# Float phases and mirrored-token sums on GpSimd, constants in parts: one change to a fused S4 convolution and GEGLU kernel

## The chip, the cores and the metric

The kernel runs on one core of a Trainium2 chip. The metric is the device time of one execution in microseconds, as a median of several runs. Engines are called by their names in the profile: PE is TensorE, DVE is VectorE, ACT is ScalarE, POOL is GpSimd, SP is SyncE, whose queue issues nearly all DMAs.

## What is computed

Two branches read the same tokens u (2048 tokens, 640 channels, bf16) and are mixed by a gate.

```python
def _A_ref(u, A_re, A_im, B_re, B_im, C_re, C_im, log_dt, Dskip):
    dt = jnp.exp(log_dt)[:, None]
    A, Bc, Cc = A_re + 1j * A_im, B_re + 1j * B_im, C_re + 1j * C_im
    P = jnp.exp((dt * A)[:, :, None] * l[None, None, :])
    K = jnp.einsum("dn,dnl,dn->dl", Cc, P, dt * Bc).real
    ...
    return y + u * Dskip[None, None, :]

def _B_ref(x, w_gate, w_up, w_down):
    return (_gelu(x @ w_gate) * (x @ w_up)) @ w_down

g = _sigmoid((x * gate_w).sum(-1, keepdims=True))
return g * a + (1 - g) * b
```

The part left out is the causal convolution y of u with K over 2048 lags, by Fourier transforms; l is 0 to 2047, rounded to bf16. A_re and the other parameters are 640 x 128; the feed-forward width is 1728.

## The kernel before, in words

The channels are worked in two halves of 320, the tokens of the feed-forward branch in two halves of 1024.

**Tables of K.** K at lag l is a sum over 128 states of a complex exponential. Each lag is written as a lag from a list of 21 ("a", `PQ`) plus a multiple of 8 up to 8 x 31 ("b", `B2`), and K comes from a product of the two tables on PE (`contract`, L515 and L516, jobs `ct`). An entry needs a magnitude (an exponential on ACT, steps `xa`, `xb`) and a cosine and a sine. The angle is built in chunks of three multiples: `phase_b` (L475) writes `th * 8m` as a 32-bit integer, of which 65536 is a full turn (step `fb`); `ph_q` (L462) reads its low 16 bits, adds a quarter turn, and writes a second integer; ACT's sine (L485 in `sin_b`, step `sb`) reads both; DVE multiplies sine and cosine by the magnitude (L503 in `prod_b`, steps `pb`, `pc`). The "a" table has the same steps: L467, L462, L479 and L494 (`fa`, `sa`, `pa`). Six b chunks (five of three multiples, one of a single one) and seven a chunks make one half of the channels. The integers live in a buffer `ph` of two slots, so a chunk's phase waits until the sine of the chunk two before has read its slot.

**Mirrored tokens.** The convolution is done in four blocks of 512 tokens by matmuls with cosine and sine matrices. For each block the tokens 256 to 511 are loaded as they are (`uf`, L354, on SP) and the tokens 255 to 0 in reverse by two indirect DMAs on POOL (`ur`, L358). The sum and the difference (L365, steps `uf0.0`, `uf0.1` and so on, bf16, 128 x 1280) go to `pm0`, which SP stores to DRAM (L366, step `us`); halves of it are loaded later (`lu`, L716). There is one `uf`, one `ur` and one `pm0`, so each block waits for the one before.

**Constants.** The matrices FM (for u, 512 KB), KMa and KMb (for K, 1 MB and 512 KB) and IM (inverse, 512 KB) are loaded by one DMA each on SP: `lfm`, `lkm`, `lkm2`, `lim`. PE uses them in L691 (jobs `U`), L704 (jobs `K`) and L764 (jobs `I`), a column block m of 128 at a time.

**Feed-forward.** PE multiplies weights with transposed tokens (L374, ten matmuls a job, jobs `g`, `u`), into one of four PSUM tiles; ACT or DVE evicts (L379, L381). Up values are spilled to DRAM through a ring of three slots (L401) and come back later (L679). Weights come through two slots of `Wr` (L270, L271 on SP). GELU, products and the down projection (L779) follow in the second part.

**What orders the work.** A string `ORDER`, written out, lists all steps; each engine and queue carries out its own instructions in that order, one after the other, and a wait holds up everything behind it. The program's names: `work`, `early` and `tail` are large SBUF buffers in which the small ones are laid out (`early` holds `uf`, `ur`, `pm0`, later FM and KMa; `work` holds `ph`).

Of the kernel before, what the change touches and what calls it, by code (L numbers as in the profile page):

```python
# [31 lines left out]
LATE = (8, 9, 10, 11)  # L32
UF = (("Uf0", "Uf1", "Uf2", "Uf3"), ("Ub0", "Uf0", "Uf1", "Uf2"))
# [6 lines left out]
al2 xb19.0 lp3 fb0.0 xb3.0 x3.0 xb11.0 xb15.0 fb1.0 xb14.0 x0.0 xb10.0 xb29.0 x1.0 xb23.0 xb21.0 xb7.0 xb9.0 lw1 t3/0  # L40
xb31.0 ur0 c3 t5/1 leu0 t4/2 x3.1 v3 xb2.0 xb12.0 v2 xa3.0 ul0 v1 xb17.0 x1.1 xa4.0 v0 xb5.0 g1.0/3 xa15.0 v5 xb13.0
leu1 x0.1 v4 xa14.0 xa8.0 u1.0/0 v6 eg1.0/D x2.1 v7 xa19.0 v8 lgw xa10.0 leu3 xa1.0 u0.0/1 eu1.0/D lsk xa9.0 v9 v11
uf0.1 xa17.0 g0.0/2 xb25.0 eu0.0/D xa5.0 v10 xb1.0 uf0.0 su1.0 xa7.0 xb4.0 v12 g2.0/3 us0 xa11.0 ur1 xb8.0 eg0.0/D
xa16.0 lw2 v13 g3.0/0 eg2.0/A x4.1 fil.0 mag v14 ma5.0 ul1 v15 ma2.0 su0.0 u3.0/1 eg3.0/A leu2 ma3.0 lu00 ma1.0 v16
ma0.0 tabT ma4.0 u2.0/2 ma6.0 v17 sb0.0 v18 u4.0/3 lw3 eu2.0/A pb0.0 sb1.0 su2.0 pc0.0 g4.0/0 uf1.0 eu3.0/A pc1.0
eu4.0/A g5.0/2 su3.0 uf1.1 at su4.0 pb1.0 us1 ur2 eg4.0/A ul2 fb2.0 gl/1 eg5.0/A fb3.0 sb2.0 u5.0/3 ph45 gl1 sb3.0
pc2.0 g6.0/0 pb2.0 lw4 eu5.0/A pb3.0 su5.0 g7.0/2 fb4.0 eg6.0/A pc3.0 sb4.0 u6.0/1 uf2.1 uf2.0 eg7.0/A fb5.0 us2 ur3
fa0.0 g8.0/3 ul3 sb5.0 eu6.0/A pb4.0 su6.0 u7.0/0 eg8.0/A pc4.0 fa1.0 sa0.0 u8.0/2 lw5 pb5.0 eu7.0/A pa0.0 u9.0/1
# [47 lines left out]
def constants():  # L96
# [37 lines left out]
    return b(fm), b(im), b(km), b(picks)  # L134


@with_exitstack
def kernel(
# [322 lines left out]
    def ph_q(t, n):  # L461
        ts(out=t[:, 1, 0:n], in0=low16(t[:, 0, 0:n])[:, :, ::2], scalar1=TURN / 4, scalar2=None, op0=ALU.add)  # L462
# [400 lines left out]
```

## Time and profile before

| | |
|---|---|
| Median of 3 runs | 295.86 us (294.83 to 297.05) |
| Profiled execution, its own time | 296.23 us |
| Its span in the profile | 294.4 us, so 1.8 us lie around it |
| Mean granted TensorE clock | 0.965 |
| POOL | 15.2 us busy in 23 instructions |

A busy row of a view gives start, duration, engine, line, operation, output <- input, shapes and count; the bracket at its end is the idle time of that engine just before, with what ended it. A row of a group gives total and mean of one. The line numbers L are those of the kernel before. A window row gives length, then for PE, PEld (weight loads), DVE, ACT and POOL the busy time and the number of instructions, then the granted clock, the share of DMA and GB/s. A label SPq is the issuing of a DMA on SP's queue.

### The profile page before, as it was taken

The numbers are of one execution on the slowest core, as the hardware profiler recorded it, in microseconds if no ns is written. First come the engines' busy times: TensorE is split into PE (matmuls) and PEld (weight loads), VectorE is DVE, ScalarE is ACT, GpSimd is POOL, SyncE is SP. The second block draws the span as 40 slices with busy tenths as digits, with TensorE's granted clock in tenths as the row PEclk, the third lists the DMA queues.
The fourth block names the chain that finished last, engine by engine and source line by source line (L and its number), as shares of the span: only waits on it lengthen the run. The fifth ranks groups of instructions, "written<-read, shape, count | busy, mean of one in ns | idle before, by whom it ended". The sixth has DMA issues, their size and how long they took to land.

```text
span 294.4 us, 4960 instructions
## 1 busy us (share of the span) xinstructions
PE 265.4 (90%) x1883; PEld 161.0 (55%) x1883; DVE 268.4 (91%) x352; ACT 215.8 (73%) x308; POOL 15.2 (5%) x23
## 2 busy tenths in 40 slices
PE   6399799999999799997098999999999999999994
PEld 4344354444584344443076446677767677677762
DVE  1599999999979879999997999999999999999993
ACT  3999978799989969999989998963764554304301
POOL 4103030200100000000001000000000000000000
PEclk9779999999999979999579999999999999999999
DMA  7996997754787893285769777844401200011001
GB/s 202 230 217 152 266 362 233 250 162 117 234 231 185 230 295 113 92 267 173 231 143 296 247 224 205 286 143 131 116 24 28 63 22 22 13 34 47 22 22 45
DMA packets 63149, 46.94 MB, mean 159 GB/s; under 512 B 23276, under 2 KB 53527, under 8 KB 62999
## 3 DMA queue, kind: packets, MB, share of 16 engines
q1 hardware_dynamic: 62166, 44.90, 54.3%
q0 software_dynamic: 384, 1.31, 1.3%
q10 hardware_dynamic: 576, 0.43, 0.5%
q8 instruction: 14, 0.23, 0.3%
q14 instruction: 9, 0.07, 0.1%
HBM read 29.39 MB, written 14.62 MB: 149 GB/s over the span
## 4 chain that ended last, share of the span: by engine, by line
DVE 63%; PE 17%; DMA 8%; ACT 4%; issue 4%; SPq 2%; ACTq 0%; DVEq 0%
DVE work L750 11%; PE ps L374 11%; DVE work L749 11%; DVE work L746 7%; DVE work L381 4%; DVE work L494 4%; DVE work L503 4%; DVE work L467 4%; DMA Wr<-in_B_w_up_dram 3%; DVE work L462 3%; DVE H L680 2%; DVE work L680 2%; DVE work L752 2%; PE ps L515 2%; PE ps L516 2%
## 5 line engine op out<-in xcount | busy, mean ns | idle before, releaser
L374 PE MATMUL ps<-xT,Wr 128*128 128x512 bf16 x540 | 121.9, 386 | 4.8 <-DMA Wr<-in_B_w_up_dram 1.9
L374 PEld LDWEIGHTS <-Wr 128*128 128x128 bf16 x540 | 53.1, 99 | 69.3 <-issue 7.4
L379 ACT CAST work<-ps 128x640 bf16<-128x640 f32 (+2 forms) x54 | 44.4, 838 | 36.3 <-PE ps L764 22.2
L750 DVE TENSOR_TENSOR work<-work 128x2560 bf16<-128x2560 bf16 x24 | 35.7, 1487 | 0.4
L779 PE MATMUL ps<-xT,work 128*128 128x320 bf16 x224 | 31.6, 299 | 0.1
L779 PE MATMUL ps<-xT,H 128*128 128x320 bf16 x224 | 31.2, 299 | 0.0
L479 ACT ACTIVATE tail<-work 128x1920 bf16<-128x1920 int16 x14 | 25.3, 1807 | 2.5 <-DVE work L503 1.7
L779 PEld LDWEIGHTS <-work 128*128 128x128 bf16 x224 | 21.9, 98 | 8.9 <-issue 0.3
L779 PEld LDWEIGHTS <-H 128*128 128x128 bf16 x224 | 21.8, 98 | 8.5
L503 DVE TENSOR_TENSOR work<-tail,work 128x1920 bf16<-128x1920 bf16 (+1 forms) x22 | 23.2, 1092 | 0.6 <-ACT tail L485 0.6
L515 PE MATMUL ps<-work 128*128 128x84 bf16 x160 | 14.1, 210 | 9.9 <-DVE work L494 9.9
L385 ACT ACTIVATE Wr<-ps,gs 128x320 bf16<-128x320 f32 x29 | 13.6, 535 | 12.4 <-PE ps L787 7.5
L485 ACT ACTIVATE tail<-work 128x960 bf16<-128x960 int16 (+1 forms) x24 | 20.7, 915 | 0.5 <-DVE work L475 0.4
L381 DVE CAST work<-ps 128x1024 bf16<-128x1024 f32 (+2 forms) x16 | 17.1, 1070 | 3.9 <-PE ps L374 2.7
L764 PE MATMUL ps<-work,tail 128*128 128x320 bf16 x128 | 19.5, 300 | 1.2 <-DVE work L431 0.6
L516 PEld LDWEIGHTS <-work 128*128 128x128 bf16 x160 | 13.6, 103 | 10.6 <-issue 10.4
L467 DVE SCALAR_TENSOR_TENSOR work<-tail 128x320 int32<-128x320 f32 x42 | 18.0, 484 | 0.0
L462 DVE TENSOR_SCALAR work<-work 128x960 int32<-128x960 int16 (+1 forms) x26 | 16.5, 636 | 1.1
L764 PEld LDWEIGHTS <-tail 128*128 128x128 bf16 x128 | 12.2, 98 | 7.2 <-issue 1.8
L691 PEld LDWEIGHTS <-early 128*128 128x128 bf16 x128 | 12.4, 98 | 6.8 <-issue 1.4
L494 DVE TENSOR_TENSOR work<-tail,work 128x1920 bf16<-128x1920 bf16 x14 | 16.0, 1152 | 0.0
L691 PE MATMUL ps<-work,early 128*128 128x320 bf16 x80 | 13.6, 299 | 1.2 <-DVE work L381 1.2
(121 smaller groups left out, 411.9 us busy)
## 6 DMA issues: line engine op xcount, KB each, us to landing
Ud<-work SPq DMA_DIRECT2D x22, 256.0 KB, 2.0
work<-Ud SPq DMA_DIRECT2D x22, 256.0 KB, 3.0
Wr<-in_B_w_gate_dram SPq DMA_DIRECT2D x12, 320.0 KB, 7.1
Wr<-in_B_w_up_dram SPq DMA_DIRECT2D x12, 320.0 KB, 4.4
PMd<-early SPq DMA_DIRECT2D x4, 640.0 KB
Gd<-work SPq DMA_DIRECT2D x9, 256.0 KB, 2.0
work<-Gd SPq DMA_DIRECT2D x9, 256.0 KB
out_dram<-Wr SPq DMA_DIRECT2D x14, 160.0 KB, 1.9
```

Of the source, the lines that this page charges most:

```text
L374: P.matmul(t[:, x, :], lhsT=Wr[:, slot, kt, cols:cols + 128], rhs=xT[:, th, kt, 512 * x:512 * x + 512], start=(kt == 0), stop=(kt == 4))
L379: A.copy(out=out, in_=in_)
L381: V.tensor_copy(out=out, in_=in_)
L462: ts(out=t[:, 1, 0:n], in0=low16(t[:, 0, 0:n])[:, :, ::2], scalar1=TURN / 4, scalar2=None, op0=ALU.add)
L467: stt(out=t[:, 0, x], in0=at["th"][:, d], scalar=float(A_OF[3 * c + x] + MID), in1=at["ph45"][:, d], op0=ALU.mult, op1=ALU.add)
L494: tt(out=PQ[:, :, 3 * c:3 * c + 3].rearrange("p r x d -> p x r d"), in0=T.rearrange("p r x d -> p x r d"), in1=e[:, :, None, :].to_broadca ...
L503: tt(out=B2[:, :, :, cols].rearrange("p r g x -> p g r x"), in0=Tv if hf == 0 else Tv[:, :, ::-1], in1=e, op=ALU.mult)
L691: P.matmul(t[:, r, 0:W2], lhsT=FM[:, e, r, 128 * m:128 * m + 128], rhs=pm[:, r, e], start=(e == 0), stop=(e == 1))
L749: step(f"m{h}{c}{i}{part}", lambda ux=ux, kx=kx: tt(out=fl(t), in0=ux, in1=kx, op=ALU.mult))
L750: step(f"s{h}{c}{i}{part}", lambda dst=dst, op=op: tt(out=fl(dst), in0=fl(dst), in1=fl(t), op=op))
L764: P.matmul(t[:, r, 0:W2], lhsT=IM[:, m, r, 128 * e:128 * e + 128], rhs=Y[:, r, m], start=(m == 0), stop=(m == 3))
L779: P.matmul(t[:, x, 0:W2], lhsT=H[c // 2][:, ft, tk:tk + 128], rhs=at[f"Wd{h}"][:, ft], start=(ft == 0), stop=False)
```

## The change

Three things change; every other step keeps its place in the list.

1. `phase_b` is split: its float part runs on POOL (`G.tensor_scalar` in place of DVE's `ts`), 16 instructions of 128 x 320 for each half of the channels. The integer part `ph_q` becomes a step of its own (`qb`, and `qa` for the a chunks, whose float part stays on DVE), directly behind `fb` or `fa`.
2. The sums and differences of mirrored tokens run on POOL (`G.tensor_tensor`), 8 instructions of 128 x 1280.
3. The constants are laid out anew on the host so that a column block is contiguous, and each load becomes several: FM 4, KMa 4, KMb 2, IM 2. These 12 DMAs stand where the 4 stood. The matmuls read the same numbers at new places.

```diff
@@ ORDER
-al2 xb19.0 lp3 fb0.0 xb3.0 x3.0 xb11.0 xb15.0 fb1.0 xb14.0 x0.0 xb10.0 xb29.0 x1.0 xb23.0 xb21.0 xb7.0 xb9.0 lw1 t3/0
+al2 xb19.0 lp3 fb0.0 qb0.0 xb3.0 x3.0 xb11.0 xb15.0 fb1.0 qb1.0 xb14.0 x0.0 xb10.0 xb29.0 x1.0 xb23.0 xb21.0 xb7.0
...
+eu12.1/D xa15.1 xa3.1 xa5.1 su12.1 xa7.1 ma1.1 xa16.1 g0.1/2 lfm0 lfm1 lfm2 lfm3 eg13.1/D kt.0 xb14.1 xa10.1 eu13.1/D
+xa19.1 xb23.1 xb4.1 ma2.1 xb2.1 xb1.1 eg0.1/D su13.1 g1.1/1 xb13.1 xb10.1 ma5.1 sg0.1 xb6.1 ma3.1 lka0 lka1 lka2 lka3
...
@@
         for r, op in ((0, ALU.add), (1, ALU.subtract)):
-            step(f"uf{c}.{r}", lambda c=c, r=r, op=op: tt(out=at["pm0"][:, r], in0=at["uf"], in1=at["ur"], op=op))
+            step(f"uf{c}.{r}", lambda c=c, r=r, op=op: G.tensor_tensor(out=at["pm0"][:, r], in0=at["uf"], in1=at["ur"], op=op))
@@ phase_b
         for x in range(n):
-            ts(out=t[:, 0, x], in0=at["th"][:, d], scalar1=8.0 * (3 * c + 1 + x), scalar2=TURN / 8, op0=ALU.mult, op1=ALU.add)
-        ph_q(t, n)
+            G.tensor_scalar(out=t[:, 0, x], in0=at["th"][:, d], scalar1=8.0 * (3 * c + 1 + x), scalar2=TURN / 8,
+                            op0=ALU.mult, op1=ALU.add)
@@ tables
+                step(f"qa{c}.{h}", lambda t=t: ph_q(t, 3))
...
+                step(f"qb{c}.{h}", lambda t=t, n=n: ph_q(t, n))
@@ loads
-    step("lfm", lambda: S.dma_start(out=at["FM"], in_=FMd))
-    step("lkm", lambda: S.dma_start(out=at["KMa"], in_=KMd[:, 0:4096]))
+    for m in range(4):
+        step(f"lfm{m}", lambda m=m: load_part("FM", FMd, m, 512))
+    for m in range(4):
+        step(f"lka{m}", lambda m=m: load_part("KMa", KAd, m, 1024))
...
+    def load_part(name, src, x, n):
+        S.dma_start(out=at[name][:, n * x:n * x + n], in_=src[:, n * x:n * x + n])
@@ u_mm
-                P.matmul(t[:, r, 0:W2], lhsT=FM[:, e, r, 128 * m:128 * m + 128], rhs=pm[:, r, e], start=(e == 0),
+                P.matmul(t[:, r, 0:W2], lhsT=FM[:, m, e, r], rhs=pm[:, r, e], start=(e == 0),
                          stop=(e == 1))
```

The compiled order shows where the moved instructions stand. In the rows of the change the line numbers are those of the changed file: L480 is `phase_b`, L364 the indirect loads, L371 the sums, L468 `ph_q`, L508 `prod_b`, L564 the step `ph45`, L603 `load_part`.

POOL's queue from its last early memset on, before:

```order
L585 MEMSET skip 32x640
L595 MEMSET H_78 64x1024
L358 DMA early<-in_A_u_dram,back 128x640 x8
L655 MEMSET xT 64x320
L543 MEMSET work 128x320
```

and the same place now:

```order
L606 MEMSET H_78 64x1024
L480 TENSOR_SCALAR work<-tail 128x320 x6
L364 DMA early<-in_A_u_dram,back 128x640 x2
L371 TENSOR_TENSOR early<-early 128x1280 x2
L364 DMA early<-in_A_u_dram,back 128x640 x2
L371 TENSOR_TENSOR early<-early 128x1280 x2
L364 DMA early<-in_A_u_dram,back 128x640 x2
L480 TENSOR_SCALAR work<-tail 128x320 x9
L371 TENSOR_TENSOR early<-early 128x1280 x2
L480 TENSOR_SCALAR work<-tail 128x320
L364 DMA early<-in_A_u_dram,back 128x640 x2
L371 TENSOR_TENSOR early<-early 128x1280 x2
```

The eight indirect loads, alone in the queue before, now alternate with the sums that read them, and the phases of chunks 2 to 5 stand between.

DVE in the first half of the channels, from the first b products to the single phase of chunk 5, before:

```order
L503 TENSOR_TENSOR work<-tail,work 128x80x2x12 x2
L365 TENSOR_TENSOR early<-early 128x1280
L503 TENSOR_TENSOR work<-tail,work 128x80x2x12
L365 TENSOR_TENSOR early<-early 128x1280
L503 TENSOR_TENSOR work<-tail,work 128x80x2x12
L475 TENSOR_SCALAR work<-tail 128x320 x3
L462 TENSOR_SCALAR work<-work 128x960
L475 TENSOR_SCALAR work<-tail 128x320 x3
L462 TENSOR_SCALAR work<-work 128x960
L559 TENSOR_SCALAR tail<-work 128x640
```

and now:

```order
L508 TENSOR_TENSOR work<-tail,work 128x80x2x12 x4
L468 TENSOR_SCALAR work<-work 128x960 x2
L564 TENSOR_SCALAR tail<-work 128x640
L508 TENSOR_TENSOR work<-tail,work 128x80x2x12 x3
L468 TENSOR_SCALAR work<-work 128x960
L508 TENSOR_TENSOR work<-tail,work 128x80x2x12
L468 TENSOR_SCALAR work<-work 128x320
```

The sums and float phases are gone from between the products; the integer phases stay where they were and take their input from POOL.

SP's queue where FM and KMa are loaded, now (before, both rows of constants were one DMA each, of 128 x 2048 and 128 x 4096):

```order
L407 DMA Ud_68<-work 128x1024
L603 DMA early<-fm_c 128x512 x4
L541 DMA KTt<-Kd_70 32x5x320 x4
L543 DMA edge_k<-Kd_70 4x320
L543 DMA edge_k<-Kd_70 6x320
L543 DMA edge_k<-Kd_70 4x320
L407 DMA Ud_68<-work 64x1024
L407 DMA Gd<-work 128x1024
L603 DMA early<-ka_c 128x1024 x4
L407 DMA Gd<-work 64x1024
```

Three issues are added ahead of K's way back from DRAM and the next spills, three more behind them.

More of the change, by code (lines that the diff above doesn't have):

```diff
@@ L44 @@
[L44 to L48, printed above, removed]
@@ L601 @@
     step("hz1", lambda: G.memset(H[1][64:128, 13], 0.0))
[L602 to L603 removed]
+    for m in range(2):
+        step(f"lkb{m}", lambda m=m: load_part("KMb", KBd, m, 1024))
+    for e in range(2):
+        step(f"lim{e}", lambda e=e: load_part("IM", IMd, e, 1024))
     def gate_mm():
```

112 lines of the change are left out of this document (59 added, 53 removed).

## The prediction, made blind

> **What bounds the kernel now.** I read the page first: the engines' busy shares and the split of the chain of waits.
>
> ```profile
> PE 265.4 (90%) x1883; PEld 161.0 (55%) x1883; DVE 268.4 (91%) x352; ACT 215.8 (73%) x308; POOL 15.2 (5%) x23
> DVE 63%; PE 17%; DMA 8%; ACT 4%; issue 4%; SPq 2%; ACTq 0%; DVEq 0%
> ```
>
> By the average, DVE is the bound and POOL is empty, so work moved from DVE to POOL ought to pay. That average hides the stages, so next come busy times by stage, for the two stretches in which the tables of K are made (first half of the channels, second half) and for the end.
>
> ```profile
> 57.30:86.20 28.90, 28.31 (x264) 16.06 (x263) 27.30 (x49) 27.59 (x27) 1.05 (x2) 1.00 0.63 183
> 109.20:147.30 38.10, 28.63 (x138) 13.36 (x137) 37.65 (x62) 36.78 (x38) 0.00 (x0) 0.91 0.57 180
> 250.00:286.00 36.00, 35.51 (x262) 25.35 (x260) 35.42 (x27) 9.18 (x18) 0.00 (x0) 1.00 0.09 28
> ```
>
> The columns after the length are PE, PEld, DVE, ACT and POOL. Where the changed work lies, three engines are full together in the first stretch, and DVE and ACT in the second (ACT idle 38.10 - 36.78 = 1.3 us). At the end PE and DVE are both full, so a lag that arrives there stays. PE's timeline says the same:
>
> ```profile
> 44.30 34.69 PE L374 MATMUL ps<-xT,Wr 128*128 128x512 bf16 x160
> 79.58 0.20 PE L515 MATMUL ps<-work 128*128 128x84 bf16 x1 [0.59 <-DVE work L494]
> 147.65 0.23 PE L515 MATMUL ps<-work 128*128 128x84 bf16 x1 [9.28 <-DVE work L494]
> ```
>
> From 44.30 to 78.99 PE runs 160 matmuls without a gap, 2.17 us for each ten. At both places where the tables end, PE waits for DVE's last product (L494): 0.59 us and 9.28 us. Faster DVE work in the first half can win at most the 0.59; in the second half it must also pass ACT, whose own waits for DVE there are these three, 1.1 us in all:
>
> ```profile
> 127.02 1.80 ACT L479 ACTIVATE tail<-work 128x1920 bf16<-128x1920 int16 x1 [0.57 <-DVE work L503]
> 135.26 1.80 ACT L479 ACTIVATE tail<-work 128x1920 bf16<-128x1920 int16 x1 [0.26 <-DVE work L462]
> 144.16 1.80 ACT L479 ACTIVATE tail<-work 128x1920 bf16<-128x1920 int16 x1 [0.26 <-DVE work L462]
> ```
>
> **The change part by part.** It takes 32 float phases (L475) and 8 sums (L365) off DVE.
>
> ```profile
> L475 DVE TENSOR_SCALAR work<-tail 128x320 int32<-128x320 f32 x32 | 8.5, 320 | 0.0
> L365 DVE TENSOR_TENSOR early<-early 128x1280 bf16<-128x1280 bf16 x8 | 6.5, 820 | 0.4 <-DMA early<-in_A_u_dram 0.3
> ```
>
> DVE is freed of 8.5 + 6.5 = 15.0 us. No row shows POOL doing arithmetic. Its nearest are memsets, one written stream:
>
> ```profile
> 0.94 0.35 POOL L544 MEMSET work<- 128x320 bf16 x1
> 2.48 0.95 POOL L595 MEMSET H<- 64x1024 bf16 x1
> ```
>
> The slope is (0.95 - 0.35)/704 = 0.85 ns an element. A phase on 320 elements costs at least 0.35 us, and at most 0.70 if read and write follow one another; I take 0.5. A sum on 1280 elements costs at least 0.35 + 960 x 0.85 ns = 1.17 us for one stream, at most 3.5 for three streams in turn; I take 2.3, the two inputs in turn, since the rows give a price for a stream and two must be read. POOL so gets 32 x 0.5 + 8 x 2.3 = 34.4 us of work.
>
> [...]
>
> *First sums.* They replace DVE work that begins at 23.08; the store that needs them, at the head of SP's queue, is the second row.
>
> ```profile
> 23.08 0.83 DVE L365 TENSOR_TENSOR early<-early 128x1280 bf16<-128x1280 bf16 x1
> 28.06 0.36 SPq L366 DMA_DIRECT2D PMd<-early  x1
> ```
>
> Starting then, POOL ends at 23.1 + 4.6 = 27.7, ahead of 28.06: nothing. At 3.5 us each it would end at 30.1, and the weight loads behind it in SP's queue would slip 2 us.
>
> *POOL's queue.* The order on POOL is fb0, fb1, load, sums, load, sums, load, then fb2 to fb4. So fb2, needed by the integer phase (L462) early in the table, stands behind the second sums and the third indirect load, and both loads that follow sums also wait for them. These rows give the clock of that queue:
>
> ```profile
> 37.83 0.83 DVE L365 TENSOR_TENSOR early<-early 128x1280 bf16<-128x1280 bf16 x1 [0.29 <-DMA early<-in_A_u_dram]
> 40.73 1.62 POOL L358 DMA_INDIRECT early<-in_A_u_dram,back  x1 [11.54 <-DVE early L365]
> 42.66 1.10 POOL L358 DMA_INDIRECT early<-in_A_u_dram,back  x1 [0.30 <-issue]
> 42.27 0.66 DVE L462 TENSOR_SCALAR work<-work 128x960 int32<-128x960 int16 x1
> 43.41 1.90 ACT L485 ACTIVATE tail<-work 128x960 bf16<-128x960 int16 x2
> 47.05 1.01 ACT L379 CAST work<-ps 128x1024 bf16<-128x1024 f32 x1
> early<-in_A_u_dram,back POOLq DMA_INDIRECT x8, 5.6
> ```
>
> The second sums can't start before their data land at 37.8. Two take until 42.4; the pair of indirect loads follows 0.3 later (POOL's own step in the third row) and takes 3.03: 45.7; fb2 three times 0.5: 47.2; DVE's integer phase 0.66: 47.9, where it ended at 42.93. DVE, relieved of three phases and two sums, reaches this point near 40 (42.27 - 0.8 - 1.6) and stands: behind it are L559 and the products L503. ACT's sine, at 43.41 in the row, starts at 47.95, 4.5 late, and the eviction behind it (47.05 in the row) ends at 52.6. PE has four PSUM tiles and wants this one back for its fifth tile, at 44.30 + 4 x 2.17 = 53.0: just covered, with 0.4 us left, so the stall goes to ACT and DVE and not yet to PE.
>
> The next knot is the single fb5 behind the third sums. fb4 waits for the sine's read (49.85) and ends at 51.35; the third loads, issued by 44.6, have landed (5.6 us) by 50.2; sums to 55.95; fb5 56.45; integer phase 56.8.
>
> ```profile
> 52.84 0.35 DVE L462 TENSOR_SCALAR work<-work 128x320 int32<-128x320 int16 x1
> 57.40 1.80 ACT L479 ACTIVATE tail<-work 128x1920 bf16<-128x1920 int16 x1 [1.10 <-DVE work L503]
> 57.44 0.38 SPq L271 DMA_DIRECT2D Wr<-in_B_w_up_dram  x1
> ```
>
> Before, it ended at 53.19: DVE is 3.6 late although it was freed of six phase groups and six sums. ACT's first joint sine, which waited for DVE in the row, starts 3.6 late. From there ACT can make up about 0.3 us (of the 1.3 idle in its stretch, part is a wait for PE's products), so PE's table products at 79.58 start **3.3 us late**. The store of the third sums slips to 56.0 in SP's queue, but the weight load behind it waits for PE until 57.44 anyway: nothing. The last pair of sums and fb0, fb1 of the second half have POOL to themselves: nothing, as long as they end inside ACT's lag.
>
> With the low prices the same steps end at 52.4, 0.8 early, of which PE can use 0.59: -0.6. With the high ones they end at 63.0: +9.8.
>
> *PE's restart.* The gap before 79.58 grows from 0.59 to about 4 us.
>
> ```profile
> 101.03 0.70 PE L691 MATMUL ps<-work,early 128*128 128x320 bf16 x4 [1.17 <-DVE work L381]
> 102.74 4.00 PE L374 MATMUL ps<-xT,Wr 128*128 128x512 bf16 x10 [1.01 <-DVE work L381]
> 109.03 2.32 PE L374 MATMUL ps<-xT,Wr 128*128 128x512 bf16 x10
> ```
>
> After gaps of 1.17 and 1.01 us, ten matmuls took 4.00 us instead of 2.32. So such a gap can cost 0 to 1.7 us: +0.8.
>
> *Second half.* Ten phases inside the stretch from 109.20 leave DVE (10 x 0.27 = 2.7 us). POOL has an empty queue, so they are ready. ACT's waits of 1.1 us are all that can be won: 0 to -1.1, I take -0.6.
>
> *Constants in parts.* Eight more issues on SP.
>
> ```profile
> 93.46 0.32 SPq L597 DMA_DIRECT2D early<-fm_c  x1
> 93.83 1.86 SPq L536 DMA_DIRECT2D KTt<-Kd  x4
> 95.74 1.00 SPq L538 DMA_DIRECT2D edge_k<-Kd  x3
> 97.21 0.49 SPq L401 DMA_DIRECT2D Ud<-work  x1
> 99.75 1.22 DVE L381 CAST work<-ps 128x1024 bf16<-128x1024 f32 x1 [0.18 <-DMA Ud<-work]
> 98.61 1.25 PE L691 MATMUL ps<-work,early 128*128 128x320 bf16 x8
> 158.39 0.91 SPq L666 DMA_DIRECT2D work<-Gd  x2
> 160.23 0.32 SPq L679 DMA_DIRECT2D work<-Ud  x1
> ```
>
> ```profile
> 173.46 0.43 SPq L603
> 173.98 0.58 SPq L716
> ```
>
> Three more issues of about 0.4 at 93.46 use up the 0.47 free before 97.21 and push that spill by 0.7; the cast at 99.75 waits for it, and PE for the next cast. +0.7 (0 to 1.7, if the three of KMa add to it). No wait gets shorter: U000 (98.61) waits for no load, and the first K product is K003, which needs the last part of KMa. The last fence is from the chain of waits, which at 173.46 runs through SP's queue; there is one issue more: +0.4 (0 to 0.45). The part of KMb goes in just before 158.39, and the gap of 0.9 before 160.23 takes it up: nothing.
>
> Sum: 3.3 + 0.8 - 0.6 + 0.7 + 0.4 = **+4.6 us** on the profiled execution's 296.23 (0.4 above the median of 295.86): **300.8 us**.
>
> **The rivals.** *Low prices, no change:* -0.6 + 0 - 0.6 + 0.7 + 0.4 = -0.1, 296.1. For it: only POOL's memsets are shown, and they are quick. Against: two operands.
>
> *Faster:* DVE alone is the bound. The chain, 63% DVE, speaks for it; ACT's 36.78 busy of 38.10 against. Then the 2.7 us freed in the second half come off PE's 9.28, with 0.6 before 79.58 and about 0.5 from the first sums, less 0.4 at SP: 296.2 - 3.4 = 292.8.
>
> *Slower still:* POOL and DVE hold each other up, each phase and sum on POOL stopping DVE for its length. In 109 to 147 that is 10 x 0.5 = 5.0 against 2.7 freed: +2.3 in place of -0.6. In 57 to 86 it is 4.6 + 3.0 = 7.6 (two sums, six phases) against 3.1 freed, less DVE's idle 1.6: +2.9. Together 300.8 + 5.8 = 306.6. No row has the two engines reading SBUF together. [...]
>
> *The parts don't do what they say:* they release nothing earlier, as worked out above; that is in the sum.
>
> **How the numbers follow.** Forecast 0.46, low prices 0.22, faster 0.13, blocking 0.19. One per cent of 295.86, about what a measurement can tell from no change, is 292.9 to 298.8. Faster by more takes the faster case, 0.13. Within it fall 0.21 of the low prices and 0.05 of the forecast with small prices: 0.26, and slower has 0.61 (0.41 + 0.19, and 0.01 from a low-price run with a slow restart). The range runs from 294.5, below the low-price case by its full -1.1 and no cost at SP, to 306.6, the blocking case; beyond lie about 0.1 on either side.
>
> **What would show it.** Right: DVE idle about 7 us before the integer phase near 47, waiting for POOL; again a wait near 56; the sine of 43.41 at 47 to 49; PE's table products at 82 to 84; POOL's sums near 2.3 us. The SP steps: the spill of 97.21 0.7 later than its neighbours' shift, and three further issues ahead of the K transfer at 174. Wrong: POOL's sums at 1.2 us and no wait for POOL on DVE; or DVE's products (L503, 1152 ns) clearly longer while POOL works, which is the blocking case; or PE's products at 79 in time and the total late, which would put the cost into SP's queue or the clock.

## The result and the profile after

The changed kernel takes 310.13 us (median of 4 runs, 308.9 to 311.83) against 296.46 us before (4 runs, 294.83 to 297.59): a ratio of 1.047, 95% interval 1.0394 to 1.0545. The forecast was 300.8 us with a range of 294.5 to 306.6: the direction was right, the size was not, and the time lies above the range. The kernel before was run again with the experiments, and each ratio there is against it on the same chip. Ratios and intervals are taken over the fast executions alone (a few over 1.5% above the fastest of their kernel are left out), medians over all, so the two can differ a little.

The profiled execution took 309.59 us. From its page, the engines' busy shares and the split of the chain of waits:

```profile
PE 268.1 (87%) x1883; PEld 161.6 (53%) x1883; DVE 275.1 (89%) x312; ACT 215.8 (70%) x308; POOL 63.8 (21%) x63
DVE 57%; SPq 10%; DMA 9%; PE 8%; ACT 6%; issue 6%; POOL 3%; DVEq 0%; ACTq 0%; POOLq 0%
```

The chain still gives DVE the largest share; SPq's part has grown because the chain now runs through the issuing of early loads up to 32 us and through POOL's second sums behind them. The mean granted clock is 0.971 against 0.965 before, so the clock is not the cause. DVE lost 40 instructions, which had taken 15.0 us, and is busier than before: 275.1 against 268.4 us. So what it kept has grown by 275.1 - (268.4 - 15.0) = **21.7 us**. Of the 13.3 us by which the span grew (294.4 to 307.7), 6.7 are DVE's busy time and 6.6 its idle time. The groups of instructions by form show which grew (the last columns are busy time, mean ns of one, and idle time before with what ended it); the last two rows are the products and integer phases before:

```profile
L371 POOL TENSOR_TENSOR early<-early 128x1280 bf16<-128x1280 bf16 x8 | 24.4, 3075 | 17.3 <-DMA early<-in_A_u_dram 14.7 <-DMA early<-in_A_u_dram,back 2.6
L508 DVE TENSOR_TENSOR work<-tail,work 128x1920 bf16<-128x1920 bf16 x20 | 31.2, 1601 | 0.1
L468 DVE TENSOR_SCALAR work<-work 128x960 int32<-128x960 int16 x24 | 21.2, 883 | 10.7 <-POOL work L480 10.0
L473 DVE SCALAR_TENSOR_TENSOR work<-tail 128x320 int32<-128x320 f32 x42 | 20.4, 541 | 0.0
L503 DVE TENSOR_TENSOR work<-tail,work 128x1920 bf16<-128x1920 bf16 x20 | 22.3, 1152 | 0.6 <-ACT tail L485 0.6
L462 DVE TENSOR_SCALAR work<-work 128x960 int32<-128x960 int16 x24 | 15.8, 660 | 1.0
```

A sum on POOL takes 3.08 us in the mean, where 2.3 was taken. The product of the table of multiples of 8 (L508, L503 before) went from 1152 to 1601 ns, the integer phase (L468, L462 before) from 660 to 883, the other table's phase (L473, L467 before) from 484 to 541. DVE also waits 10.0 us for POOL, which it never did.

To see where, cut the span at points that both kernels pass: DVE's first product for the b table, the end of chunk 2's integer phase, ACT's first joint sine (L479, L484 after: sine and cosine in one instruction), PE's first table product of either half, and the end. Four of the six windows of the trace after, with the columns as in the prediction, and behind them the second and third of the trace before:

```profile
0.00:36.80 36.80, 26.42 (x146) 14.72 (x147) 24.81 (x32) 30.93 (x54) 16.73 (x22) 1.00 0.98 213
36.80:50.30 13.50, 13.50 (x135) 7.19 (x133) 9.78 (x6) 7.09 (x9) 11.12 (x8) 1.00 0.87 268
50.30:68.00 17.70, 11.40 (x44) 4.61 (x43) 16.20 (x16) 10.59 (x15) 14.52 (x11) 0.90 0.42 128
68.00:93.89 25.89, 21.48 (x91) 9.22 (x90) 24.68 (x33) 21.31 (x17) 9.58 (x7) 0.93 0.44 135
35.30:42.90 7.60, 7.09 (x54) 3.55 (x55) 7.28 (x12) 5.98 (x8) 1.86 (x2) 1.00 1.10 330
42.90:57.40 14.50, 14.50 (x123) 7.35 (x120) 13.69 (x25) 11.64 (x15) 3.00 (x3) 1.00 0.74 249
```

Before, the six stretches lasted 35.30, 7.60, 14.50, 22.18, 68.07 and 146.75 us; after, the last two last 67.06 and 146.75. The loss is +1.5, +5.9, +3.2 and +3.7 us in the first four, 14.3 in all, then -1.0 and 0.0. Everything that was lost was lost before PE's table products, which began at 93.89 and not 79.58.

From POOL's timeline after, the rows between 20 and 62 us on which the reading rests:

```profile
21.85 5.43 POOL L371 TENSOR_TENSOR early<-early 128x1280 bf16<-128x1280 bf16 x2 [7.00 <-DMA early<-in_A_u_dram]
38.31 6.64 POOL L371 TENSOR_TENSOR early<-early 128x1280 bf16<-128x1280 bf16 x2 [7.66 <-DMA early<-in_A_u_dram]
48.12 6.58 POOL L480 TENSOR_SCALAR work<-tail 128x320 int32<-128x320 f32 x9
54.78 6.86 POOL L371 TENSOR_TENSOR early<-early 128x1280 bf16<-128x1280 bf16 x2
```

And from DVE's timeline over the same time:

```profile
22.70 2.11 DVE L346 TENSOR_SCALAR work<-work 128x640 f32<-128x640 f32 x1
24.73 1.21 DVE L387 CAST work<-ps 128x1024 bf16<-128x1024 f32 x1
25.87 2.10 DVE L347 SCALAR_TENSOR_TENSOR work<-work 128x640 f32<-128x640 f32 x1
36.78 9.18 DVE L508 TENSOR_TENSOR work<-tail,work 128x1920 bf16<-128x1920 bf16 x4
49.68 0.66 DVE L468 TENSOR_SCALAR work<-work 128x960 int32<-128x960 int16 x1 [3.72 <-POOL work L480]
59.11 3.05 DVE L468 TENSOR_SCALAR work<-work 128x960 int32<-128x960 int16 x1
63.40 0.31 DVE L468 TENSOR_SCALAR work<-work 128x320 int32<-128x320 int16 x1
```

Read the two side by side. While the first sums run (21.85 to 27.28), a scaling of 0.48 us takes 2.11 and a multiply-add of 0.82 takes 2.10, but the cast between them, whose input is in PSUM, takes its usual 1.21. While the second sums run (38.31 to 44.95), four products take 9.18 us instead of about 4.5. At 59.11 an integer phase takes 3.05 us instead of 0.66. None of these instructions waits for POOL: their rows show no idle time ended by it, and the phases that the one at 59.11 reads were ready at 54.70. The 3.72 at 49.68 is a wait of the other kind, for a phase that stands in POOL's queue behind the second sums and two indirect loads.

ACT and PE then hand the lag on:

```profile
49.68 1.90 ACT L490 ACTIVATE tail<-work 128x960 bf16<-128x960 int16 x2 [5.99 <-POOL work L480]
67.92 1.80 ACT L484 ACTIVATE tail<-work 128x1920 bf16<-128x1920 int16 x1 [1.22 <-DVE work L508]
```

```profile
64.20 10.48 PE L380 MATMUL ps<-xT,Wr 128*128 128x512 bf16 x40 [5.14 <-ACT H L385]
77.67 14.80 PE L380 MATMUL ps<-xT,Wr 128*128 128x512 bf16 x60 [2.99 <-ACT work L385]
93.89 0.20 PE L520 MATMUL ps<-work 128*128 128x84 bf16 x1 [1.42 <-DVE work L499]
```

PE, which ran 160 matmuls without a gap before, now waits 5.14 and 2.99 us for ACT to free PSUM.

### The profile page after: what moved, and what is told of

Its sections match the earlier page's. It is cut to its first block, busy times and chain, and to the rows that moved or that the text cites. A ratio compares the mean times of both kernels' runs of the same rounds, so it can differ in the third digit from the quotient of the medians.

```text
span 307.7 us, 4978 instructions
## 1 busy us (share of the span) xinstructions
PE 268.1 (87%) x1883; PEld 161.6 (53%) x1883; DVE 275.1 (89%) x312; ACT 215.8 (70%) x308; POOL 63.8 (21%) x63
## 3 DMA queue, kind: packets, MB, share of 16 engines
q0 software_dynamic: 384, 1.31, 1.6%
## 4 chain that ended last, share of the span: by engine, by line
DVE 57%; SPq 10%; DMA 9%; PE 8%; ACT 6%; issue 6%; POOL 3%; DVEq 0%; ACTq 0%; POOLq 0%
DVE work L765 11%; DVE work L764 11%; DVE work L761 7%; SPq L284 6%; DVE work L473 5%; DVE work L468 4%; DVE work L508 4%; PE ps L380 4%; DVE work L499 3%; ACT tail L484 2%; POOL early L371 2%; DVE H L695 2%; DMA early<-ka_c 2%; DMA early<-in_A_u_dram 2%; DVE work L695 2%
## 5 line engine op out<-in xcount | busy, mean ns | idle before, releaser
L380 PE MATMUL ps<-xT,Wr 128*128 128x512 bf16 x540 | 124.6, 390 | 13.6 <-ACT H L385 5.1
L380 PEld LDWEIGHTS <-Wr 128*128 128x128 bf16 x540 | 53.8, 100 | 80.1 <-issue 20.3
L480 POOL TENSOR_SCALAR work<-tail 128x320 int32<-128x320 f32 x32 | 23.6, 738 | 44.7 <-ACT tail L490 22.4
L508 DVE TENSOR_TENSOR work<-tail,work 128x1920 bf16<-128x1920 bf16 (+1 forms) x22 | 32.1, 1499 | 0.1
L468 DVE TENSOR_SCALAR work<-work 128x960 int32<-128x960 int16 (+1 forms) x26 | 21.7, 839 | 10.7 <-POOL work L480 10.0
L484 ACT ACTIVATE tail<-work 128x1920 bf16<-128x1920 int16 x14 | 25.4, 1813 | 6.5 <-DVE work L508 5.7
L371 POOL TENSOR_TENSOR early<-early 128x1280 bf16<-128x1280 bf16 x8 | 24.4, 3075 | 17.3 <-DMA early<-in_A_u_dram 14.7
L391 ACT ACTIVATE Wr<-ps,gs 128x320 bf16<-128x320 f32 x29 | 13.7, 536 | 12.4 <-PE ps L802 7.5
L473 DVE SCALAR_TENSOR_TENSOR work<-tail 128x320 int32<-128x320 f32 x42 | 20.4, 541 | 0.0
L521 PEld LDWEIGHTS <-work 128*128 128x128 bf16 x160 | 13.6, 104 | 11.5 <-issue 11.4
L499 DVE TENSOR_TENSOR work<-tail,work 128x1920 bf16<-128x1920 bf16 x14 | 16.5, 1187 | 0.0
```

The lines of the kernel that those rows point to most:

```text
L371: step(f"uf{c}.{r}", lambda c=c, r=r, op=op: G.tensor_tensor(out=at["pm0"][:, r], in0=at["uf"], in1=at["ur"], op=op))
L380: P.matmul(t[:, x, :], lhsT=Wr[:, slot, kt, cols:cols + 128], rhs=xT[:, th, kt, 512 * x:512 * x + 512], start=(kt == 0), stop=(kt == 4))
L473: stt(out=t[:, 0, x], in0=at["th"][:, d], scalar=float(A_OF[3 * c + x] + MID), in1=at["ph45"][:, d], op0=ALU.mult, op1=ALU.add)
L484: act(out=T, in_=low16(t)[:, :, :, ::2], func=ACT.Sin, scale=SIN_SCALE)
L499: tt(out=PQ[:, :, 3 * c:3 * c + 3].rearrange("p r x d -> p x r d"), in0=T.rearrange("p r x d -> p x r d"), in1=e[:, :, None, :].to_broadca ...
L508: tt(out=B2[:, :, :, cols].rearrange("p r g x -> p g r x"), in0=Tv if hf == 0 else Tv[:, :, ::-1], in1=e, op=ALU.mult)
```

## The experiments

Two theories stood against each other. **Queue**: phases and loads stand behind the sums on POOL and come late. **Exclusion**: POOL and DVE cannot use SBUF at the same time, so POOL's work stops DVE wherever it runs.

### One part of the change at a time

The change has three parts. Each was made alone in the kernel before. The constants in parts (the layout and loads of the change, and no other line of it):

```diff
-    step("lfm", lambda: S.dma_start(out=at["FM"], in_=FMd))
+    for m in range(4):
+        step(f"lfm{m}", lambda m=m: load_part("FM", FMd, m, 512))
...
```

> Only the constants in parts; phases and sums stay on DVE as before. Queue theory and blocking theory alike: POOL has no new work, so nothing of the 13.7 us should appear. The prediction had put +1.1 us on SP's queue (0.7 at FM, 0.4 at IM); the trace of the changed kernel shows the stretch with those loads no longer than before, so by that 0 +- 1 us. If it is +1 or more, the eight issues are a cost that the trace hides behind the other lag.

298.06 us against 296.81 (12 and 23 runs), ratio 1.0039 (1.0006 to 1.0072). The size is the +1.1 of the prediction, but its trace doesn't put it where I did: the stretch between PE's two table products, with all the loads of FM and KMa, is 67.56 us against 68.07 before, and the products begin 1.6 us late, ahead of the first changed load. Executions of the kernel before differ among themselves by more than that (293.5 to 299.39), so one trace can't place it. The cause of this 1 us stays open.

The phases on POOL alone:

```diff
-            ts(out=t[:, 0, x], in0=at["th"][:, d], scalar1=8.0 * (3 * c + 1 + x), scalar2=TURN / 8, op0=ALU.mult, op1=ALU.add)
+            G.tensor_scalar(out=t[:, 0, x], in0=at["th"][:, d], scalar1=8.0 * (3 * c + 1 + x), scalar2=TURN / 8, op0=ALU.mult, op1=ALU.add)
```

> Only the 32 float phases on POOL; sums on DVE, constants whole. Queue theory (time is lost because phases stand behind sums and indirect loads in POOL's queue): only the indirect loads are left ahead of chunk 2, so DVE waits about 3 us there and +2 to +4 us in all, with DVE's products at their old 1152 ns. Blocking theory (a POOL instruction that reads SBUF and a DVE instruction that does so stop each other): some 22 phases of 0.5 us stand beside DVE work in the full stretches, 11 us against 8.5 freed, plus the same wait: +3 to +6 us, with DVE's products and integer phases lengthened while POOL works.

298.94 us against 296.81, ratio 1.0086 (1.0045 to 1.0127), though DVE waits 9.5 us for POOL's phases. The interval, +1.3 to +3.8 us, reaches into the ranges of both theories, so the time does not decide between them. DVE's remaining work has grown by 264.0 - (268.4 - 8.5) = 4.1 us, 0.13 for each phase, and its products from 1152 to 1238 ns. The wait is long to look at and costs little here because DVE is rid of 8.5 us of phases in exchange.

The sums on POOL alone:

```diff
-            step(f"uf{c}.{r}", lambda c=c, r=r, op=op: tt(out=at["pm0"][:, r], in0=at["uf"], in1=at["ur"], op=op))
+            step(f"uf{c}.{r}", lambda c=c, r=r, op=op: G.tensor_tensor(out=at["pm0"][:, r], in0=at["uf"], in1=at["ur"], op=op))
```

> Only the 8 sums on POOL; phases on DVE, constants whole. No DVE or ACT instruction waits for a sum, and SP's stores of them have slack. Queue theory: -0.6 to +1 us. Blocking theory: 8 sums of 2.7 us (21.8 us) stop DVE for nearly their whole length, 6.5 us of DVE work are freed, and the first pair falls where DVE has idle time: +5 to +10 us, with DVE's L503, L467 and L462 two to three times as long while a sum runs.

307.27 us against 296.81, ratio 1.0323 (1.0279 to 1.0367): +10.5 us by the medians, +9.6 by the ratio, although no instruction of DVE or ACT waits for POOL. The three parts add up: 0.0039 + 0.0086 + 0.0323 = 0.045, against 0.047 for the change. The page of this kernel:

```profile
PE 267.1 (87%) x1868; PEld 161.6 (53%) x1883; DVE 280.2 (92%) x344; ACT 215.9 (71%) x308; POOL 39.0 (13%) x31
```

DVE's remaining work has grown by 280.2 - (268.4 - 6.5) = 18.3 us. PE waits 5.4 us for weights in this trace (1.9 before), and how much of that comes from stores behind the sums in SP's queue is not separated here; the spare additions below have no such store. Two rows of its DVE timeline beside two pairs of sums (39.33 to 46.22 and 67.87 to 73.65):

```profile
36.98 6.78 DVE L503 TENSOR_TENSOR work<-tail,work 128x1920 bf16<-128x1920 bf16 x4
67.88 6.11 DVE L467 SCALAR_TENSOR_TENSOR work<-tail 128x320 int32<-128x320 f32 x3
```

Three phases that took 1.29 us together take 6.11.

### POOL's queue in another order

The changed kernel, with fb2 and fb3 ahead of the second sums and fb5 ahead of the third:

```diff
-lu00 ma1.0 v16 ma0.0 tabT ma4.0 u2.0/2 ma6.0 v17 sb0.0 v18 u4.0/3 lw3 eu2.0/A pb0.0 sb1.0 su2.0 pc0.0 g4.0/0 uf1.0
-eu3.0/A pc1.0 eu4.0/A g5.0/2 su3.0 uf1.1 at su4.0 pb1.0 us1 ur2 eg4.0/A ul2 fb2.0 qb2.0 gl/1 eg5.0/A fb3.0 qb3.0 sb2.0
-u5.0/3 ph45 gl1 sb3.0 pc2.0 g6.0/0 pb2.0 lw4 eu5.0/A pb3.0 su5.0 g7.0/2 fb4.0 qb4.0 eg6.0/A pc3.0 sb4.0 u6.0/1 uf2.1
-uf2.0 eg7.0/A fb5.0 qb5.0 us2 ur3 fa0.0 qa0.0 g8.0/3 ul3 sb5.0 eu6.0/A pb4.0 su6.0 u7.0/0 eg8.0/A pc4.0 fa1.0 qa1.0
+lu00 ma1.0 v16 ma0.0 tabT ma4.0 u2.0/2 ma6.0 v17 sb0.0 v18 u4.0/3 lw3 eu2.0/A pb0.0 sb1.0 fb2.0 fb3.0 su2.0 pc0.0 g4.0/0 uf1.0
+eu3.0/A pc1.0 eu4.0/A g5.0/2 su3.0 uf1.1 at su4.0 pb1.0 us1 ur2 eg4.0/A ul2 qb2.0 gl/1 eg5.0/A qb3.0 sb2.0
+u5.0/3 ph45 gl1 sb3.0 pc2.0 g6.0/0 pb2.0 lw4 eu5.0/A pb3.0 su5.0 g7.0/2 fb4.0 qb4.0 eg6.0/A pc3.0 sb4.0 u6.0/1 fb5.0 uf2.1
+uf2.0 eg7.0/A qb5.0 us2 ur3 fa0.0 qa0.0 g8.0/3 ul3 sb5.0 eu6.0/A pb4.0 su6.0 u7.0/0 eg8.0/A pc4.0 fa1.0 qa1.0
```

> All of the change, but in POOL's queue the phases of chunks 2 and 3 go ahead of the second sums, and the phase of chunk 5 ahead of the third sums, so that no phase stands behind a sum any more. Queue theory: the two knots at 47.9 and 56.8 of the prediction are gone, at least 7 of the 13.7 us come back: 301 to 303 us. Blocking theory: POOL's work is the same and still stops DVE for its length: 306 to 309 us, and DVE's waits for POOL (10.0 us in the changed kernel) fall while its products get longer.

308.05 us, ratio 1.0378 (1.0323 to 1.0432): about 2 us of the 13.7 come back, and even that is not sure, since the interval overlaps that of the change (1.0394 to 1.0545). At least 7 would have had to, by the queue theory. DVE's wait for POOL falls from 10.0 to 6.5 us, but L473, which now meets the sums, goes from 541 to 713 ns in the mean. The hold moves to other instructions. The queue theory falls as the main cause.

### Work on POOL that nobody waits for

The kernel before, with four additions that nothing reads, placed in POOL's queue behind the last indirect loads (step `dz`; the memset `dm` stands near the start):

```diff
...
+    step("dm", lambda: G.memset(KTt[:, 0:2], 1.0))
+    def spare():
+        for i in range(4):
+            G.tensor_tensor(out=KTt[:, 2:4], in0=KTt[:, 0:2], in1=KTt[:, 0:2], op=ALU.add)
...
+    step("dz", spare)
```

> The kernel before, with four more additions of 128x1280 bf16 on POOL behind the last of its indirect loads of the first half. They add a tile of ones to itself, nobody reads their result, and no instruction waits for them but POOL's own next ones; DVE keeps all its work. If only lateness on POOL's queue costs, the time stays within 0.5 us of before. If POOL and DVE hold each other up whenever both read SBUF, the additions of 2.7 us each take DVE's time in full: +7 to +11 us, and DVE's products near them read 2 to 3.5 us instead of 1.15.

306.51 us against 297.78, ratio 1.0295 (1.0238 to 1.0352). The additions ran for 11.25 us from 57.03. Its DVE timeline there, and its page:

```profile
56.80 6.77 DVE L503 TENSOR_TENSOR work<-tail,work 128x1920 bf16<-128x1920 bf16 x2
63.50 5.53 DVE L467 SCALAR_TENSOR_TENSOR work<-tail 128x320 int32<-128x320 f32 x3
```

```profile
PE 268.3 (88%) x1883; PEld 161.4 (53%) x1883; DVE 277.5 (91%) x352; ACT 216.0 (71%) x308; POOL 27.0 (9%) x28
```

DVE grew by 9.1 us and the time by 8.7, with no other step moved, and no instruction of another engine near them uses their result. This shows exclusion as a cause by itself.

The same place with four memsets (`G.memset(KTt[:, 0:5], 1.0)` for the addition):

> The same place and about the same length of POOL time, but four memsets of 128x3200 bf16 (some 2.8 us each by the slope of the memset rows), which read nothing. If reading SBUF is what shuts DVE out, nothing: within 0.5 us of before. If any POOL instruction that touches SBUF does it, writes too, +7 to +11 us as with the additions.

303.1 us against 297.78, ratio 1.0183 (1.012 to 1.0246): neither of the two numbers. The DVE timeline beside them (57.77 to 69.80):

```profile
57.05 4.01 DVE L462 TENSOR_SCALAR work<-work 128x960 int32<-128x960 int16 x1
60.98 2.21 DVE L503 TENSOR_TENSOR work<-tail,work 128x1920 bf16<-128x1920 bf16 x2
63.12 1.28 DVE L467 SCALAR_TENSOR_TENSOR work<-tail 128x320 int32<-128x320 f32 x3
64.50 2.60 DVE L462 TENSOR_SCALAR work<-work 128x960 int32<-128x960 int16 x1
```

The two-input instructions L503 and L467 run at their old speed beside POOL's memsets (two products in 2.21 us and three phases in 1.28, 2.22 and 1.28 in the trace before); the integer phase L462, with one input, is held, twice, by 3.35 and 1.94 us. Together that is 5.3, and the time grew by 5.3. So "reads" alone was too narrow.

### The conflict by itself

A kernel of nothing else, each kind of DVE instruction six times, alone and beside POOL (the whole of its loop):

```python
for k in ("add", "phase", "zero"):
    for o in ("tt", "stt", "ts", "ti", "cast"):
        V.memset(cover(k), 1.0)
        pool(k)
        for _ in range(6):
            dve(o)
        V.memset(left(k), 1.0)
```

> Not the kernel: it computes nothing of the reference and writes ones. It runs five kinds of DVE instruction six times each, alone and then beside POOL additions (two of 128x1280 bf16), POOL phases (ten of 128x320 float to integer) and POOL memsets (two of 128x3200). Theory of exclusion by reads: beside the additions the products, the fused multiply-adds and the float scalings grow by about as much in all as the additions last (one of them by 2 us or more), the casts out of PSUM stay at 1.2 us, and beside the memsets all stay as alone. Rival, a slower shared port: every DVE instruction that touches SBUF grows by a like share, beside memsets too.

Rows of its timeline, alone first (products, float scalings, casts, two additions, ten phases), then DVE and POOL together: with the additions, with the phases (all ten, and the six of them that lie beside the products), with the memsets.

```profile
19.98 7.06 DVE L62 TENSOR_TENSOR b<-b,b 128x1920 bf16<-128x1920 bf16 x6
32.11 3.13 DVE L66 TENSOR_SCALAR f<-f 128x640 f32<-128x640 f32 x6
39.20 7.51 DVE L70 CAST b<-ps 128x1024 bf16<-128x1024 f32 x6
46.94 5.28 POOL L75 TENSOR_TENSOR g<-g,g 128x1280 bf16<-128x1280 bf16 x2 [40.93 <-DVE g L99]
52.57 5.35 POOL L78 TENSOR_SCALAR gi<-gf 128x320 int32<-128x320 f32 x10 [0.35 <-DVE gf L99]
64.01 11.60 DVE L62 TENSOR_TENSOR b<-b,b 128x1920 bf16<-128x1920 bf16 x6
64.18 6.84 POOL L75 TENSOR_TENSOR g<-g,g 128x1280 bf16<-128x1280 bf16 x2 [0.35 <-DVE g L104]
85.35 7.65 DVE L66 TENSOR_SCALAR f<-f 128x640 f32<-128x640 f32 x6
101.75 7.45 DVE L70 CAST b<-ps 128x1024 bf16<-128x1024 f32 x6
109.27 7.73 DVE L62 TENSOR_TENSOR b<-b,b 128x1920 bf16<-128x1920 bf16 x6
109.44 10.06 POOL L78 TENSOR_SCALAR gi<-gf 128x320 int32<-128x320 f32 x10 [2.19 <-DVE gf L104]
109.44 7.88 POOL L78 TENSOR_SCALAR gi<-gf 128x320 int32<-128x320 f32 x6 [2.19 <-DVE gf L104]
149.33 7.09 DVE L62 TENSOR_TENSOR b<-b,b 128x1920 bf16<-128x1920 bf16 x6
162.70 8.11 DVE L66 TENSOR_SCALAR f<-f 128x640 f32<-128x640 f32 x6
```

In a table, the time that POOL's work added to six DVE instructions (us):

| six DVE instructions | alone | + 2 additions (5.28) | + 10 phases (5.35) | + 2 memsets (5.59) |
|---|---|---|---|---|
| products, two SBUF inputs | 7.06 | +4.54 | +0.67 | +0.03 |
| multiply-adds, two SBUF inputs | 5.12 | +4.49 | +0.58 | -0.06 |
| float scalings, one input | 3.13 | +4.52 | +0.59 | +4.98 |
| integer phases, one input | 4.13 | +4.48 | +0.59 | +4.98 |
| casts from PSUM | 7.51 | -0.06 | -0.06 | -0.05 |

Three things follow. Beside the additions the loss is the same for all four kinds of instruction with inputs in SBUF (+4.48 to +4.54 us), so it is POOL's time that is added and not a share of DVE's: 4.5 us for a pair of additions. The casts from PSUM lose nothing (-0.06 to -0.05 us). And the phases, as long in all as the additions, cost DVE only 0.6. That column needs care, though. Only six of the ten phases lie beside the six products, one to each, and they take 7.88 us, 1.31 each instead of 0.54 alone: POOL and DVE take turns. So a phase holds DVE for some 0.67 / 6 = 0.1 us, and a product holds a phase for longer, 1.31 - 0.54 = 0.8 us.

The 4.5 a pair accounts for the runs above: four pairs of sums make 18.0 us (18.3 measured as the growth of DVE's work in the kernel with the sums alone), four spare additions 9.0 (9.1 measured). Less the 6.5 us that DVE is freed of, the sums should cost 11.5; the run showed 10.5 by the medians.

Of the 5.28 us that two additions take alone, DVE loses 4.5: nearly all, but not the whole. The memsets (5.59 us) hold the one-input scalings and integer phases by 4.98 us and the two-input products and multiply-adds by nothing (+0.03 and -0.06); why they differ, no run shows. Casts out of PSUM were tried, casts from SBUF were not.

### Long or short, two inputs or one

The probe again with other lengths (eight additions of 320 elements, three phases of 1280, twenty memsets of 160):

```diff
...
-                G.tensor_tensor(out=g[2][:], in0=g[0][:], in1=g[1][:], op=ALU.add)
+                for x in range(4):
+                    d = slice(320 * x, 320 * x + 320)
+                    G.tensor_tensor(out=g[2][:, d], in0=g[0][:, d], in1=g[1][:, d], op=ALU.add)
...
```

> Not the kernel, and ones as its output: the first probe with other lengths on POOL. The two additions are cut into eight of 128x320, the ten phases become three of 128x1280, the memsets twenty of 128x160. In the first probe additions of 2.6 us cost DVE's six instructions +4.5 us, phases of 0.53 us only +0.6. If the length of a POOL instruction decides (each hold has a part that DVE can run under), the short additions cost DVE under 2 us and the long phases 3 us or more. If the kind decides (two inputs against one), the short additions still cost about +4.5 and the long phases about +0.6.

From its timeline, the eight additions and three phases alone, then the float scalings beside each, with six of the additions that ran beside the first:

```profile
46.94 5.99 POOL L77 TENSOR_TENSOR g<-g,g 128x320 bf16<-128x320 bf16 x8 [40.14 <-DVE g L101]
53.02 3.94 POOL L80 TENSOR_SCALAR gi<-gf 128x1280 int32<-128x1280 f32 x3
77.17 5.88 DVE L66 TENSOR_SCALAR f<-f 128x640 f32<-128x640 f32 x6
77.69 6.01 POOL L77 TENSOR_TENSOR g<-g,g 128x320 bf16<-128x320 bf16 x6
118.83 5.89 DVE L66 TENSOR_SCALAR f<-f 128x640 f32<-128x640 f32 x6
```

Against 3.13 alone that is +2.75 beside the short additions and +2.76 beside the long phases. The short additions too take turns with DVE, one to each scaling (six in 6.01 us, six scalings in 5.88), so the loss is 2.75 / 6 each. By the single POOL instruction, DVE loses 2.25 of 2.64 us (long addition), 0.92 of 1.31 (long phase), 0.46 of 0.75 (short addition) and 0.1 of 0.53 (short phase): **its length less 0.3 to 0.4 us**, for additions and phases alike. The multiply-adds and the integer phases give the same within 0.05 us. The products lost 1.40 beside the short additions, because POOL was still at its memsets until 60.8 us and only three of the six products, which began at 57.69, met an addition: 3 x 0.46 = 1.4. They lost 3.20 beside the long phases, because one short addition ran on until 101.10 into products that began at 100.60: 3 x 0.92 + 0.4 = 3.2. Twenty short memsets (3.52 us in all) cost the scalings nothing (3.07 us). In all, the short additions are over the 2 us that the theory of length gave and far under the 4.5 of the theory of kind; the long phases, at 2.8, are just under its 3 and far from 0.6. Of the two, it is length.

Does that mend the change? The sums in four pieces each, in the kernel with the sums alone and in the changed kernel:

```diff
...
+                for y in range(2):
+                    for z in (0, 320):
+                        G.tensor_tensor(out=at["pm0"][:, r, y, z:z + 320], in0=at["uf"][:, y, z:z + 320],
+                                        in1=at["ur"][:, y, z:z + 320], op=op)
...
```

> The kernel before with the eight sums on POOL, each cut into four of 128x320. Sums in one piece cost +10.5 us. If the length of a POOL instruction decides, DVE runs on between the pieces and the time is between -1 and +3 us of before. If the kind decides, DVE is held for the same length in smaller portions: +8 to +11 us.

308.13 us against 296.97, ratio 1.0397 (1.0313 to 1.0481).

> The changed kernel with each sum cut into four of 128x320, nothing else changed. If the length decides, what the sums cost (10.5 of 13.7 us) goes for the most part, though POOL's queue is no shorter: 298 to 303 us. If the kind decides, 308 to 311 us as the change has it.

313.37 us, ratio 1.0563 (1.0495 to 1.063). Both are misses for the theory of length as a remedy: the first, +11.2 us, is just above what the theory of kind gave, the second above either. Neither can be told from its counterpart with whole sums, since the intervals overlap. The expectation asked too much of the pieces. At 0.46 each, 32 pieces hold DVE for 14.7 us where eight whole sums hold it for 18.0, so some 3 us could be won. With the pieces DVE's remaining work grew by 16.5 us in the kernel with the sums alone (18.3 with whole sums), and by 12.8 in the changed kernel (21.7). What is won seems to be lost in POOL's time; the traces suggest it, and no run tests it by itself. A pair of sums takes 7.2 to 9.0 us, where its data are there, instead of 5.4 to 6.9. In the kernel with the sums alone, the store that needs the first pair goes out at 30.33 instead of 27.52, the weight loads stand behind it in SP's queue, and PE waits for them:

```profile
38.39 8.50 PE L380 MATMUL ps<-xT,Wr 128*128 128x512 bf16 x29 [5.43 <-DMA Wr<-in_B_w_up_dram]
```

With the sums whole that wait was 3.09 us. In the changed kernel DVE's wait for POOL's phases doubles, from 10.0 to 19.6 us, which takes back the 8.9 by which its work grew less.

### The second half alone

The float phases of the second half on POOL, where its queue is empty:

```diff
-            ts(out=t[:, 0, x], in0=at["th"][:, d], scalar1=8.0 * (3 * c + 1 + x), scalar2=TURN / 8, op0=ALU.mult, op1=ALU.add)
+            (G.tensor_scalar if h == 1 else ts)(out=t[:, 0, x], in0=at["th"][:, d], scalar1=8.0 * (3 * c + 1 + x), scalar2=TURN / 8, op0=ALU.mult, op1=ALU.add)
```

> The kernel before with the float phases of the second half alone on POOL (16 of the 32, nothing else changed). By the prediction's term for the second half, -0.6 us: POOL's queue is empty there. If each phase on POOL stops DVE for its length, 16 x 0.5 = 8 us of stops against 16 x 0.27 = 4.3 us freed, of which the table stretch has ten: +2.3 us at most. The changed kernel's second segment, 0.5 us shorter, speaks for the first.

297.27 us against 297.78 (12 and 17 runs), ratio 1.0013 (0.998 to 1.0046): no difference that the runs can tell, while the +2.3 us of a stop for each phase's full length lies outside the interval (-0.6 to +1.4 us). No version tried is faster than the kernel before.

## Why the prediction was wrong, point by point

**What bounds the kernel** was read rightly: three engines full together in the first stretch, so that a lag there stays. It arrived at the end undiminished: the last stretch is 146.75 us in both kernels.

**The step that failed is the price of POOL's work to DVE: nothing.** The sum let POOL's instructions run beside DVE's and counted only when their results come. Exclusion stood among the rivals, with 0.19 and 306.6 us. That POOL's work holds DVE up was right; the rival's price for it was too low. It counted two stretches from 57.3 and 109.2 on, so only the last pair of sums, though three of the four pairs begin before 57.3. (It was added up from stops of a POOL instruction's full length, which no run shows: a sum's hold of 2.3 us was about right, 2.25 of 2.64 measured; a phase's of 0.5 was too much, 0.1 of 0.53 in the probe and 0.13 in the kernel with the phases alone.) With eight sums at 2.25, 18.0 us held less 6.5 freed, it would have given +11.5 for the sums alone. The windows of before, shown beside those of after, could have told that these places have no slack: DVE was busy for 7.28 of the 7.60 us from 35.30 and for 13.69 of the 14.50 from 42.90, where the second and the third pair lie. Of the signs named, the one for blocking came: the products went from 1152 to 1601 ns. DVE's idle time before the integer phase near 47 was 3.72 us and not 7, and no wait came near 56, because stretched products filled that time.

**The direction** came out right partly by luck. The forecast's main term, lateness in POOL's queue with 3.3 us, is a small part of the loss: the phases alone, with their waits, cost about 2 us, and the other order gave back about 2, where the sums alone cost 10.

**Prices.** The phase alone was right: 0.53 us for 0.5 taken. The sum was low: 2.64 alone for 2.3, and beside DVE it is 3.08 in the mean, since POOL too is held (in the probe a pair of additions takes 5.28 us alone and 6.84 beside the products).

**First sums: nothing.** They ended at 27.28, ahead of their store at 27.89, as worked out. But they held a scaling and a multiply-add by 1.6 and 1.3 us, against 1.6 us that DVE was freed of there; the first stretch is 1.5 us longer, which that step did not have.

**POOL's queue** went in the order worked out and each step came late. The second sums began at 38.31 (37.8 forecast) and ended at 44.95 (42.4); the integer phase ended at 50.3 (47.9); ACT's sine began at 49.68 (47.95); the single phase behind the third sums came so late that its integer phase ended at 63.7 (56.8); ACT's first joint sine began 10.5 us late (3.6), PE's table products 14.3 (3.3). Up to 50 the lag beyond the forecast, 2.4 us, is that the sums took 6.64 us and not 4.6; behind that, it is DVE being held: from 52.99 on, three products and an integer phase take 9.2 us, where 3 x 1.15 + 0.66 = 4.1 was usual. That "fb2 behind the sums" is not the heart of it is shown by the other order, which gave back about 2 us.

**PE's restart**, +0.8, does not appear: the stretch from 93.89 is 1.0 us shorter than before, although the gap ahead of it grew (0.59 to 1.42 us, where 4 was forecast). **Second half**, -0.6: within that -1.0; the run of that part alone could not tell it from nothing. **Constants in parts**, +0.7 and +0.4: the run alone gave +1.2 (0.2 to 2.1), but neither place shows it, so its size is borne out, perhaps by luck, and its mechanism is not. The stretch with the last of those loads is unchanged.

## What to carry to other kernels

The sums moved from VectorE to GpSimd were not taken off VectorE, since they ran long beside its work in SBUF (6.5 us freed, 18.3 us of growth in its other work): as measured in the two probes, take the length of each addition or phase on GpSimd less 0.3 to 0.4 us as time that VectorE loses, and subtract what was freed. A sum took GpSimd 2.64 us alone and VectorE 0.82, so the move loses 2.25 - 0.82 = 1.4 us a sum even where nothing waits for the result. Cutting the sums into four won nothing here. Such work cost little where VectorE evicts PSUM (the casts of the probe, -0.06 us beside two additions), or where the GpSimd instructions are short and nobody waits for them (0.1 us for a phase of 0.53, though still 0.46 for an addition of 0.75); a wait for GpSimd in the profile (10.0 us here) is the smaller sign, and the larger is VectorE's own instructions growing (21.7 us).

## What the runs showed of the hardware that I had not expected

That the loss is the same for all four kinds of DVE instruction tried with inputs in SBUF (4.48 to 4.54 us beside a pair of additions), so a short one is stretched most: 0.32 to 2.7 us in the kernel with the sums alone. That POOL's memsets, which read nothing, hold the one-input scalings (3.13 to 8.11 us) and leave the two-input products alone (7.06 and 7.09). And that POOL is held as well: short phases and products took turns, one phase every 1.31 us instead of 0.54, and the product lost only 0.1 us each time.
